# Capped attention and a spatial gating block on one Trainium2 core: the low parts of the weights move from GpSimd to VectorE, and the list scheduler in the source is given that exclusion and new weights

## The chip, the cores and the metric

The kernel runs on one core of one Trainium2 chip. The metric is the device time of one execution in microseconds, as the median of several executions. The core has TensorE (PE) for matmuls, VectorE (DVE), ScalarE (ACT), GpSimd (POOL) and SyncE (SP), which here issues almost all DMAs. The profile is of one execution.

## The reference

Four batches; each has 12 attention heads over 448 positions with 64 values a head, and then a gated block on the 768 joined values.

```python
def _attn_ref(q, k, v, cap):                       # (4, 12, 448, 64) each
    scores = cap * np.tanh(scale * q @ k.T / cap)
    attn = np.exp(scores - max);  attn /= attn.sum + 1e-9
    return attn @ v

def _moe_ref(x, w_in, g_ln, w_sg, b_sg, w_out):    # x (4, 448, 768)
    h = gelu_tanh(x @ w_in)                        # 768 -> 1024
    u, v = h[..., :512], h[..., 512:]
    v_n = (v - mean) / sqrt(var + 1e-6) * g_ln
    v_s = einsum('ts,bsd->btd', w_sg, v_n) + b_sg  # 448 x 448 over positions
    return x + (u * v_s) @ w_out                   # 512 -> 768
```

`w_in` and `w_out` come as 64-bit floats and are taken apart on the chip. (The lines above are shortened from the reference; the max is taken out of the kernel's work, since the cap bounds the scores.)

## The kernel before

**Precision by splitting.** Most matmuls run in a rounded 32-bit format. Each operand is kept as a high part (a rounded copy) and a low part (the value minus that copy), and a product is three matmuls: high x high, high x low, low x high (`TERMS`). So everything that enters such a matmul costs a copy (helper `cop`, on VectorE at L323 or ScalarE at L325, whichever the scheduler chooses) and a subtraction.

**Attention.** A batch has six pairs of heads, in three groups of two pairs. `split` makes the high and low parts of q and k (L323/L325 and L525). A group has seven units: six of 128 keys of one pair, and one for the last 64 keys of both pairs. A unit is: scores on TensorE (L535, the tail unit L543) into one of two PSUM tiles `sc`; tanh (L596) and exp (L598) on ScalarE into a tile `p`; the product with v (L554, tail L564) into an accumulator `ps`; and the row sums (`den`, L479), also on TensorE. Where `SUMS` is true for the batch, VectorE first adds three units of a pair together (L615), so that a group needs three entries in `den` and not seven; two entries make one `den` operation of eight matmuls.

**The gated block of a batch, `gated(b)`.** `recip` turns `den` into reciprocals (VectorE L625 to L631). `norm` multiplies each of the six x tiles by them (a matmul L656 that spreads them, VectorE L659) and splits x (L662, L665). Then TensorE runs `hv` (v half of x @ w_in, L698), `hu` (u half, L745), `vsg` (L762) and `outp` (L784), with gelu (L679 to L686), statistics (L717 to L730, of which L722 on GpSimd) and further splits between them.

**Weights.** `decode` handles one chunk of `w_in` (twelve of 128x512) or `w_out` (eight of 128x384): a DMA of the 64-bit words into a tile `stage`, then L395 or L397, L401, L405 and L410 on VectorE or ScalarE, an integer addition on GpSimd (L415), the high copy (L422) and the low part by a subtraction on GpSimd (L423). `split_sg` does copy and subtraction (L458, GpSimd) for the four chunks of `w_sg`. No `hv` can finish before the six chunks of the v half are decoded.

**What sets the order.** The program first collects all operations with their buffers (`Plan.op`), each with a key. `Plan.run` is a list scheduler in the source: it keeps a modelled time for each engine, and takes again and again the operation that could start first; among those of one engine within 0.04 us of each other the lowest key wins. It issues the instructions in that order, so each engine's queue is fixed when the program is built, and on the chip an engine works it off in order. The modelled costs are `c_act`, `c_tt`, `c_ts`, `c_pool`, `mms`. A DMA is modelled as 0.065 us of SP. GpSimd's hold on VectorE enters only in one place: a VectorE operation marked `fast` is lengthened by at most 0.36 us while GpSimd is busy. Keys come from the constants at the top: attention unit i has `akey(i)` (5.0 + 0.43 i for the first 42 units, then a pitch of 1.82 from 132.71); the gated blocks start at `MOE + MOE_SPAN * b`.

Of the kernel before, what the change touches and what calls it, by code (L numbers as in the profile page):

```python
# [22 lines left out]
FIRST_PITCH = 0.43  # L23
SECOND = 132.71
ATT_PITCH = 1.82
MOE = 103.44
MOE_SPAN = 49.4
SWITCH = 5.7
SIZES = (3, 7, 4, 3, 14)
RS = 19  # L30
G_CAP = 3
ACT_SH = 71.76
DVE_SH = 22.15
# [9 lines left out]
SG_FETCH = (50.0, 3.0)  # L43
GELU = 9.94
NORM = 53.2
RECIP = 20.57
VAL = 4.3
DEN = 0.0
DEC_AHEAD = 12.02

LAT = {
    ("pe", "pe"): 0.0, ("pe", "act"): 0.04, ("pe", "dve"): 0.04, ("pe", "sp"): 0.03,
# [21 lines left out]
def c_pool(n):  # L74
    return 0.0028 * n + 0.15
# [55 lines left out]
class Plan:  # L131
# [35 lines left out]
    def run(self):  # L167
        engines = ("pe", "act", "dve", "pool", "sp")
        free = dict.fromkeys(engines, 0.0)
        cand = {e: [] for e in engines}  # L170
        mode, wire, left = None, 0.0, len(self.ops)

        def ready(o):
            for e in o.engs:
                cand[e].append(o)

        for o in self.ops:
            if not o.npred:
                ready(o)
        while left:  # L180
            best = None
            for e in engines:
                ests, f = [], free[e]
# [16 lines left out]
                pick = min(  # L200
                    (x for x in ests if x[0] <= first),
                    key=lambda x: (x[1].key + (SWITCH if e == "pe" and x[1].mode != mode else 0.0)
                                   + ({"act": ACT_SH, "dve": DVE_SH}[e] if len(x[1].engs) > 1 else 0.0), x[1].num))
                if best is None or pick[0] < best[0]:
                    best = (*pick, e)
            if best is None:
                raise RuntimeError(f"stuck with {left} left")
            t, o, e = best
            cost, fn = o.engs[e]
            for k in o.engs:  # L210
                cand[k].remove(o)
            for b in o.alloc:
                b.pool.take(b)
            if e == "pe":
                if mode != o.mode:
# [14 lines left out]
            left -= 1  # L230
            for s in o.weak:
                s.npred -= 1
                s.ready = max(s.ready, t)
                if not s.npred:
                    ready(s)
            for s in o.succ:
                s.npred -= 1
                s.ready = max(s.ready, t if e == "pe" and "pe" in s.engs else max(end + LAT[e, k] for k in s.engs))
                if not s.npred:
                    ready(s)  # L240
            for b in o.bufs:
                b.left -= 1
                b.end = max(b.end, end)
                if not b.left and b.pool is not None:
                    b.pool.give(b)
        return max(free.values())
# [3 lines left out]
def kernel(  # L250
# [61 lines left out]
    ps_p = Pool([pp.tile([128, 512], FP32, name=f"ps{i}") for i in range(3)], {"g": G_CAP})  # L312
# [26 lines left out]
    def load(out, in_, buf, size, key, rd=()):  # L339
        return op("sp", 0.065, lambda: nc.sync.dma_start(out=out(), in_=in_), rd=rd, wr=[buf], key=key, size=size)  # L340

    def akey(i):
        n = 2 * NU * NG
        return i * FIRST_PITCH + 5.0 if i < n else SECOND + (i - n) * ATT_PITCH

# [6 lines left out]
    load(lambda: cap_sb, cap.partition_broadcast(128), k_cap, 512, 1.0)  # L352
# [25 lines left out]
    def decode(name, ws, src, c, sl, key):  # L378
# [10 lines left out]
        op("sp", 0.065, lambda: nc.sync.dma_start(out=st.t[:, :2 * n].bitcast(U64), in_=src),  # L389
# [23 lines left out]
        def whole():  # L413
# [39 lines left out]
    def split_sg(c):  # L453
# [12 lines left out]
    def attention(b):  # L466
# [3 lines left out]
        total = NG * (NU if not SUMS[b] else 3)  # L470
# [22 lines left out]
        def group(gi):  # L493
# [7 lines left out]
            pav = [Buf(ps_p, cls="a") for _ in pairs]  # L501
# [5 lines left out]
            def fetch(s):  # L507
                for n, src in enumerate((q2, k2)):
                    op("sp", 0.065, lambda s=s, n=n, src=src: nc.sync.dma_start(
                        out=raw[s].t[:, n, :], in_=src[b, pairs[s]]),  # L510
                       wr=[(raw[s], n)], key=base - FETCH_G + s * 3, size=128 * S * 4)

            def fetch_v(s):
                op("sp", 0.065, lambda: nc.sync.dma_start(out=v[s].t, in_=vp[b, pairs[s]]),
                   wr=[v[s]], key=base - 12 + 12 * s, size=128 * 128 * FC * 4)

            def split(s):
                key = akey(i0 + (FC + 1) * s) - SPLIT
                parts = range(2) if g == 0 and s == 0 else (slice(0, 2),)
                for n in parts:  # L520
# [4 lines left out]
                    op("dve", c_tt(cols), lambda n=n: nc.vector.tensor_tensor(  # L525
                        out=hl[s].t[:, 1, n], in0=raw[s].t[:, n], in1=f32(hl[s].t[:, 0, n]), op=ALU.subtract),
                       rd=[(raw[s], reg), (hl[s], ("h", n) if reg is not None else "h")],
                       wr=[(hl[s], ("l", n) if reg is not None else "l")], key=key)
# [50 lines left out]
            op("sp", 0.065, lambda: nc.sync.dma_start(out=vtail.t, in_=vt[b, gi]),  # L579
# [4 lines left out]
            for k, (s, c) in enumerate(units):  # L584
# [22 lines left out]
                if not SUMS[b]:  # L607
# [14 lines left out]
    def recip(b, key):  # L622
# [8 lines left out]
        op("dve", c_tt(S), lambda: nc.vector.tensor_tensor(  # L631
            out=rds[64:], in0=t.t[:64, :S], in1=f32(rds[:64]), op=ALU.subtract),
           rd=[t, (k_rds, 0)], wr=[(k_rds, 1)], key=key - RECIP)

    def gated(b):
        start = MOE + MOE_SPAN * b
# [14 lines left out]
        def norm(p):  # L653
# [8 lines left out]
            op("dve", c_tt(S), lambda: nc.vector.tensor_tensor(  # L662
                out=xl[p].t[:, :S], in0=xr[p].t, in1=f32(xh[p].t[:, :S]), op=ALU.subtract),
               rd=[xr[p], (xh[p], 0)], wr=[xl[p]], key=k)
# [27 lines left out]
        def hv(t):  # L692
# [35 lines left out]
            def lo():  # L728
# [5 lines left out]
            op("dve", c_tt(HF), lambda: nc.vector.tensor_tensor(  # L734
                out=lo(), in0=vv(), in1=f32(vh[t].t[:n]), op=ALU.subtract),
               rd=[v2, (vh[t], 0)], wr=[vl[t] if t < FC else (vh[t], 1)], key=key + 1)
# [18 lines left out]
        def vsg(f):  # L755
            ps = Buf(ps_p, cls="g")
            for c in range(NC):
# [17 lines left out]
            op("dve", c_tt(S), lambda: nc.vector.tensor_tensor(  # L775
                out=gl[f].t[:, :S], in0=uu[f].t, in1=f32(gh[f].t[:, :S]), op=ALU.subtract),
               rd=[uu[f], gh[f]], wr=[gl[f]], key=key)

        def outp(c):
# [13 lines left out]
            op("sp", 0.065, lambda: nc.sync.dma_start(out=outT[b, c], in_=x.t), rd=[x], key=key, size=128 * S * 4)  # L793
# [82 lines left out]
```

## Time and profile before

| | |
|---|---|
| median of 3 runs | 418.34 us (417.82 to 449.83) |
| the profiled execution's own time | 417.94 us |
| its span, first to last instruction | 416.2 us |
| PE busy | 391.9 us (94%), 2144 matmuls |
| DVE busy | 312.0 us (75%) |
| ACT busy | 238.6 us (57%) |
| POOL busy | 78.8 us (19%), 64 instructions |
| mean granted TensorE clock | 0.987 |

A row of instruction groups gives the line and engine, what is written and read with its shape, the count, then busy time, mean duration in ns and the idle time of the engine just before them with what ended it. A windows row gives busy us and instruction counts of each engine in a stretch. A row of the chain gives start, length and the work that the end of the kernel hung on at that moment. Matmuls overlap, so a matmul's mean duration is longer than its share of the engine's time; the chain's merged rows give that share. Likewise two VectorE instructions in a row overlap by some 0.08 us.

### The profile page before, as it was taken

To read this page: it belongs to the slowest core of one execution; us is meant where nothing else is said; L and a number is where in the kernel's file an instruction comes from. 1 tells how busy PE (TensorE), PEld (TensorE's weight loads), DVE (VectorE), ACT (ScalarE), POOL (GpSimd) and SP (SyncE) were. 2 spreads that over 40 slices of the span, in tenths; PEclk is the share of its full clock that TensorE was granted. 3 is DMA by queue.
4 is the path that set the end of the run, shared out by engine and by line. 5 is a ranking of instruction groups with operands and counts; after the bars stand their busy time and mean duration, and the time that the engine had idled before them with its cause. 6 is when DMAs were issued, how large, how long until landed. Compare 5 with 4: busy or idle time off the path is not lost.

```text
span 416.2 us, 5637 instructions
## 1 busy us (share of the span) xinstructions
PE 391.9 (94%) x2144; PEld 258.3 (62%) x2144; DVE 312.0 (75%) x515; ACT 238.6 (57%) x314; POOL 78.8 (19%) x64
## 2 busy tenths in 40 slices
PE   4988979689899999999999999999999999999996
PEld 1333424223467994856657747568557989889995
DVE  2899999989999789755686985962289967278551
ACT  5998897929577545485476575752833423134210
POOL 0443472856612322100010000000000100011000
PEclk9999999869999999999999999999999999999999
DMA  7992560605212122241030030211000001100012
GB/s 251 338 346 89 166 228 16 206 8 164 63 45 83 44 72 66 84 130 52 21 106 8 20 113 20 63 46 66 2 22 0 2 0 60 53 22 2 1 45 89
DMA packets 20140, 33.42 MB, mean 80 GB/s; under 512 B 2960, under 2 KB 17424, under 8 KB 20112
## 3 DMA queue, kind: packets, MB, share of 16 engines
q1 hardware_dynamic: 20112, 33.05, 24.3%
q8 instruction: 17, 0.28, 0.3%
q14 instruction: 11, 0.09, 0.1%
HBM read 27.53 MB, written 5.51 MB: 79 GB/s over the span
## 4 chain that ended last, share of the span: by engine, by line
PE 67%; DVE 18%; issue 5%; DMA 4%; POOL 3%; ACT 1%; SPq 1%; DVEq 0%; ACTq 0%; POOLq 0%
PE ps L698 12%; PE ps L784 10%; PE ps L745 8%; PE ps L554 7%; PE ps L762 6%; PE sc L535 6%; PE sc L784 4%; PE sc L745 4%; PE sc L762 2%; DMA stage<-in_w_in_dram 2%; DVE stage L410 2%; POOL win L423 2%; DVE t L628 2%; PE den L479 2%; PE sc L698 2%
## 5 line engine op out<-in xcount | busy, mean ns | idle before, releaser
L596 ACT ACTIVATE p<-sc,qsc 128x896 f32<-128x896 f32 x84 | 81.2, 1008 | 35.1 <-PE sc L535 29.8
L598 ACT ACTIVATE p<-p,cap_sb 128x896 f32<-128x896 f32 x84 | 84.1, 1046 | 0.2
L554 PE MATMUL ps<-p,v 128*64 128x448 f32 x276 | 59.2, 553 | 0.8 <-ACT p L598 0.7
L535 PE MATMUL sc<-hl 64*128 64x448 f32 x432 | 58.8, 393 | 0.5 <-ACT p L596 0.5
L535 PEld LDWEIGHTS sc<-hl 64*128 64x128 f32 x432 | 37.2, 188 | 34.3 <-ACT p L596 13.5
L615 DVE TENSOR_TENSOR p<-p,p 128x896 f32<-128x896 f32 x36 | 43.2, 1200 | 7.8 <-PE ps L554 6.5
L722 POOL TENSOR_TENSOR sm<-sm,pw 128x1 f32<-128x1 f32 (+1 forms) x16 | 9.3, 580 | 209.9 <-DVE sm L719 209.9
L698 PE MATMUL ps<-win,rg 128*128 128x512 f32 x187 | 47.7, 397 | 0.0
L745 PE MATMUL ps<-rg,win 128*128 128x448 f32 x202 | 45.0, 367 | 0.0
L784 PE MATMUL ps<-rg,wout 128*128 128x448 f32 x198 | 44.2, 369 | 0.0
L415 POOL TENSOR_TENSOR stage<-stage 128x512 int32<-128x512 int32 (+1 forms) x20 | 30.4, 1518 | 62.4 <-DVE stage L410 46.8
L698 PEld LDWEIGHTS ps<-win,rg 128*128 128x128 f32 x187 | 34.7, 188 | 9.8 <-issue 1.4
L745 PEld LDWEIGHTS ps<-rg,win 128*128 128x128 f32 x202 | 37.7, 188 | 4.8 <-issue 0.7
L784 PEld LDWEIGHTS ps<-rg,wout 128*128 128x128 f32 x198 | 36.8, 188 | 5.7 <-issue 1.7
L554 PEld LDWEIGHTS ps<-p,v 128*64 128x64 f32 x276 | 16.9, 137 | 32.6 <-issue 23.6
L679 ACT ACTIVATE t<-ps 128x448 f32<-128x448 f32 (+1 forms) x22 | 12.5, 568 | 38.0 <-PE ps L698 28.6
L479 PE MATMUL den<-p,ones_sb 128*32 128x448 f32 x192 | 27.1, 567 | 4.8 <-DVE t L625 3.1
L684 ACT ACTIVATE t<-t 128x448 f32<-128x448 f32 (+2 forms) x32 | 19.4, 605 | 20.7 <-DVE t L681 20.6
L681 DVE SCALAR_TENSOR_TENSOR t<-t,ps 128x448 f32<-128x448 f32 (+1 forms) x22 | 14.2, 645 | 22.6 <-ACT t L679 22.5
L423 POOL TENSOR_TENSOR win<-stage,win 128x512 fp32r<-128x512 f32 x12 | 25.4, 2120 | 25.7 <-DVE win L323 23.6
L525 DVE TENSOR_TENSOR hl<-raw,hl 128x896 fp32r<-128x896 f32 (+1 forms) x25 | 26.8, 1075 | 1.5 <-ACT hl L325 1.3
L762 PE MATMUL ps<-wsg,rg 128*128 128x448 f32 x111 | 24.4, 367 | 0.0
(117 smaller groups left out, 536.0 us busy)
## 6 DMA issues: line engine op xcount, KB each, us to landing
stage<-in_w_in_dram SPq DMA_DIRECT2D x12, 512.0 KB, 5.6
raw<-in_q_dram SPq DMA_DIRECT2D x24, 224.0 KB, 3.6
raw<-in_k_dram SPq DMA_DIRECT2D x24, 224.0 KB, 3.9
out_dram<-x SPq DMA_DIRECT2D x24, 224.0 KB, 1.9
v<-in_vp_dram SPq DMA_DIRECT2D x24, 192.0 KB, 2.7
stage<-in_w_out_dram SPq DMA_DIRECT2D x8, 384.0 KB, 3.2
u<-in_w_sgT_dram SPq DMA_DIRECT2D x4, 224.0 KB, 7.5
vt<-in_vt_dram SPq DMA_DIRECT2D x12, 64.0 KB, 2.3
```

What stands on the lines that cost most here:

```text
L415: nc.gpsimd.tensor_tensor(out=a.bitcast(I32), in0=a.bitcast(I32), in1=hi, op=ALU.add)
L423: op("pool", c_pool(n), lambda: nc.gpsimd.tensor_tensor(out=ws[1][:, c, sl], in0=words()[2], in1=f32(ws[0][:, c, sl]), op=ALU.subtract), r ...
L479: nc.tensor.matmul(out=den.t[32 * j:32 * j + 32, :S], lhsT=ones_sb[:, kind, NP - 1 - kind - p:NP + 31 - kind - p], rhs=src.t[:, h, :], sta ...
L535: nc.tensor.matmul(out=sc.t[:, h, :S], lhsT=hl[s].t[rows, w, 1, 128 * c - 128:128 * c], rhs=hl[s].t[rows, m, 0], start=(k == 0), stop=(k = ...
L554: nc.tensor.matmul(out=pav[s].t[64 * h:64 * h + 64, :S], lhsT=v[s].t[:, 128 * (c - 1) + 64 * h:128 * (c - 1) + 64 * h + 64], rhs=p.t[:, h, ...
L596: op("act", c_act(2 * S, True, True), lambda p=p, sc=sc: nc.scalar.activation(out=p.t, in_=sc.t[:, :, :S], func=ACTF.Tanh, scale=qsc), rd= ...
L598: op("act", c_act(2 * S, False, True), lambda p=p: nc.scalar.activation(out=p.t, in_=p.t, func=ACTF.Exp, scale=cap_sb), rd=[k_cap], wr=[p] ...
L615: op("dve", c_tt(2 * S), lambda a=a, p=p: nc.vector.tensor_tensor(out=a.t, in0=a.t, in1=p.t, op=ALU.add), rd=[p], wr=[a], key=akey(i) + 5.0)
L698: nc.tensor.matmul(out=ps.t[:, :HF], lhsT=(xl if a else xh)[c].t[:, t * 128:t * 128 + 128], rhs=win[w][:, c, HF:], start=(c == 0 and k == ...
L745: nc.tensor.matmul(out=ps.t[:, :S], lhsT=win[w][:, c, f * 128:(f + 1) * 128], rhs=(xl if a else xh)[c].t[:, :S], start=(c == 0 and k == 0) ...
L762: nc.tensor.matmul(out=ps.t[:, :S], lhsT=(vl if a else vh)[c].t[:, f * 128:(f + 1) * 128], rhs=wsg[w][:, c, :], start=(c == 0 and k == 0), ...
L784: nc.tensor.matmul(out=ps.t[:, :S], lhsT=wout[w][:, f, c * 128:(c + 1) * 128], rhs=(gl if a else gh)[f].t[:, :S], start=(f == 0 and k == 0 ...
```

## The change

The two low-part subtractions of the weights go to VectorE, through a new helper `sub` that also serves the subtractions already there. The scheduler now treats a marked VectorE operation and a GpSimd operation as exclusive, in both directions, and gets new costs for GpSimd and for a DMA issue. Two DMAs of k at the start go to ScalarE's queue. `SUMS` is now per group, the attention keys per batch, the start and span of each gated block per batch, and nearly all other constants, buffer counts among them, have new values.

```diff
-FIRST_PITCH = 0.43
-SECOND = 132.71
-ATT_PITCH = 1.82
-MOE = 103.44
-MOE_SPAN = 49.4
-SWITCH = 5.7
-SIZES = (3, 7, 4, 3, 14)
+ATT = ((-2.4, 2.04), (48.67, 2.63), (116.23, 4.59), (190.0, 4.4))
+GATED = ((68.97, 119.99), (182.94, 117.55), (316.07, 26.93), (334.53, 60.0))
+SWITCH = 6.88
+SIZES = (3, 5, 4, 3, 18)
...
-SUMS = (True, False, True, True)
-RETIRE = (8, 8, 8, 8, 8, 0)
-IN_V = (22.2, 15.3)
-IN_U = (36.4, 5.3)
-OUT_W = (136.5, 12.2)
-SG_W = (57.5, 5.9)
-FETCH_W = 38.96
-FETCH_G = 38.23
-SPLIT = 19.18
...
+SUMS = (0, 1, 0, 0, 1, 0, 1, 1, 1, 1, 1, 1)
+RETIRE = (11, 8, 7, 8, 8, 0)
+IN_V = (33.7, 15.2)
+IN_U = (51.1, 6.6)
+OUT_W = (145.9, 10.0)
+SG_W = (64.9, 4.1)
+FETCH_W = 8.26
+FETCH_G = 8.66
+SPLIT = 37.4
...
+ISSUE = 0.45
...
 def c_pool(n):
-    return 0.0028 * n + 0.15
+    return 0.00235 * n + 0.09
...
+        port = {"dve": 0.0, "pool": 0.0}
...
                 for o in cand[e]:
                     t = o.ready if o.ready > f else f
+                    if o.fast and e in port:
+                        t = max(t, port["dve" if e == "pool" else "pool"])
...
             else:
-                if e == "dve" and o.fast:
-                    cost += 0.6 * max(0.0, min(free["pool"], t + 0.6) - t)
                 end = t + cost
+                if o.fast and e in port:
+                    port[e] = end - 0.135
                 free[e] = end - OVERLAP[e]
...
-    ps_p = Pool([pp.tile([128, 512], FP32, name=f"ps{i}") for i in range(3)], {"g": G_CAP})
+    ps_p = Pool([pp.tile([128, 512], FP32, name=f"ps{i}") for i in range(3)], {"g": G_CAP, "b": 2})
...
+    def sub(out, a, b, n, rd, wr, key):
+        op("dve", c_tt(n), lambda: nc.vector.tensor_tensor(out=out(), in0=a(), in1=b(), op=ALU.subtract),
+           rd=rd, wr=wr, key=key, fast=True)
...
-        op("pool", c_pool(n), whole, rd=[(st, "h")], wr=[(st, "a")], key=key)
+        op("pool", c_pool(n), whole, rd=[(st, "h")], wr=[(st, "a")], key=key, fast=True)
         cop(lambda: ws[0][:, c, sl], lambda: words()[2], n, [(st, "a")], [(w, 0)], key)
-        op("pool", c_pool(n), lambda: nc.gpsimd.tensor_tensor(
-            out=ws[1][:, c, sl], in0=words()[2], in1=f32(ws[0][:, c, sl]), op=ALU.subtract),
-           rd=[(st, "a"), (w, 0)], wr=[(w, 1)], key=key)
+        sub(lambda: ws[1][:, c, sl], lambda: words()[2], lambda: f32(ws[0][:, c, sl]), n,
+            [(st, "a"), (w, 0)], [(w, 1)], key)
...
-        op("pool", c_pool(S), lambda: nc.gpsimd.tensor_tensor(
-            out=wsg[1][:, c, :], in0=u.t, in1=f32(wsg[0][:, c, :]), op=ALU.subtract),
-           rd=[u, (w, 0)], wr=[(w, 1)], key=SG_W[0] + SG_W[1] * c)
+        sub(lambda: wsg[1][:, c, :], lambda: u.t, lambda: f32(wsg[0][:, c, :]), S,
+            [u, (w, 0)], [(w, 1)], SG_W[0] + SG_W[1] * c)
...
                 for n, src in enumerate((q2, k2)):
-                    op("sp", 0.065, lambda s=s, n=n, src=src: nc.sync.dma_start(
+                    eng = "act" if n and not g else "sp"
+                    queue = nc.scalar if n and not g else nc.sync
+                    op(eng, ISSUE, lambda s=s, n=n, src=src, queue=queue: queue.dma_start(
                         out=raw[s].t[:, n, :], in_=src[b, pairs[s]]),
...
                     def to_ps(bf):
                         ps_p.caps = {}
-                        for z in range(2):
-                            ps_p.add(bf.end, bf.t[:, z, :])
+                        ps_p.add(bf.end, bf.t[:, 0, :])
                         return True
...
-                if not SUMS[b]:
+                if not SUMS[g]:
...
-                        out=a.t, in0=a.t, in1=p.t, op=ALU.add), rd=[p], wr=[a], key=akey(i) + 5.0)
+                        out=a.t, in0=a.t, in1=p.t, op=ALU.add), rd=[p], wr=[a], key=akey(i) + 5.0, fast=True)
...
-        start = MOE + MOE_SPAN * b
+        start, span = GATED[b]
```

## Rows read from the trace of the kernel before

**Rows 1.** Windows, four stretches: engine busy us (instructions), TensorE clock, DMA share, GB/s.
```profile
0.00:60.00 60.00, 50.95 (x314) 19.80 (x314) 50.07 (x76) 52.26 (x59) 24.88 (x14) 1.00 0.73 242
60.00:112.00 52.00, 42.10 (x277) 15.96 (x278) 49.23 (x67) 36.25 (x45) 29.88 (x21) 0.90 0.28 88
112.00:310.00 198.00, 197.11 (x1076) 133.61 (x1074) 144.10 (x249) 121.17 (x161) 20.17 (x23) 1.00 0.18 58
```

**Rows 2.** Chain that ended last, pieces in which TensorE runs without a gap.
```profile
133.38 14.72 PE ps L745 x72
...
239.09 0.91 PE sc L543 x8
...
246.58 0.91 PE ps L564 x8
...
248.29 0.89 PE den L479 x8
249.18 2.41 PE ps L554 x12
251.58 1.43 PE sc L535 x12
...
363.60 7.69 PE ps L698 x33
```

**Rows 3.** What TensorE waited for before 112 us: total, times, longest.
```profile
PE ps L656 <- DVE x L659: 6.2, 1, 6.2
PE sc L543 <- DMA raw<-in_k_dram: 5.2, 1, 5.2
PE den L479 <- DVE t L625: 3.1, 1, 3.1
```

**Rows 4.** Windows of 10 us around the longest wait, same columns as rows 1.
```profile
80.00:90.00 10.00, 4.69 (x21) 1.43 (x23) 10.00 (x13) 3.68 (x5) 6.96 (x5) 0.55 0.14 50
90.00:100.00 10.00, 10.00 (x70) 3.87 (x68) 7.46 (x15) 7.77 (x9) 5.68 (x4) 0.94 0.26 74
```

**Rows 5.** Instruction groups on GpSimd, whole span.
```profile
L415 POOL TENSOR_TENSOR stage<-stage 128x512 int32<-128x512 int32 (+1 forms) x20 | 30.4, 1518 | 62.4 <-DVE stage L410 46.8 <-DVE stage L405 15.2 <-issue 0.4
...
L423 POOL TENSOR_TENSOR win<-stage,win 128x512 fp32r<-128x512 f32 x12 | 25.4, 2120 | 25.7 <-DVE win L323 23.6 <-ACT win L325 2.1
...
L423 POOL TENSOR_TENSOR wout<-stage,wout 128x384 fp32r<-128x384 f32 x8 | 8.3, 1040 | 4.5 <-ACT wout L325 3.2 <-DVE wout L323 1.3
...
L458 POOL TENSOR_TENSOR wsg<-u,wsg 128x448 fp32r<-128x448 f32 x4 | 5.7, 1439 | 0.0
```

**Rows 6.** Timeline, all engines: a subtraction on GpSimd among VectorE's instructions (start, length).
```profile
27.43 2.07 POOL L423 TENSOR_TENSOR win<-stage,win 128x512 fp32r<-128x512 f32 x1 [2.77 <-DVE win L323]
...
28.28 2.17 DVE L615 TENSOR_TENSOR p<-p,p 128x896 f32<-128x896 f32 x1
...
30.91 1.08 DVE L615 TENSOR_TENSOR p<-p,p 128x896 f32<-128x896 f32 x1
```

**Rows 7.** Instruction groups on VectorE, 0 to 112 us.
```profile
L615 DVE TENSOR_TENSOR p<-p,p 128x896 f32<-128x896 f32 x12 | 17.1, 1427 | 0.2 <-ACT p L596 0.2
...
L410 DVE SCALAR_TENSOR_TENSOR stage<-stage 128x512 int32<-128x512 int32 (+1 forms) x14 | 13.1, 941 | 0.1
L401 DVE TENSOR_SCALAR stage<-stage 128x512 f32<-128x512 f32 (+1 forms) x14 | 10.6, 756 | 0.6 <-POOL win L423 0.6
L405 DVE TENSOR_SCALAR stage<-stage 128x512 int32<-128x512 int32 (+1 forms) x14 | 9.4, 675 | 0.0
```

**Rows 8.** VectorE's timeline: the decode's steps where GpSimd is not at work.
```profile
71.33 0.41 DVE L401 TENSOR_SCALAR stage<-stage 128x512 f32<-128x512 f32 x1
...
90.20 0.41 DVE L405 TENSOR_SCALAR stage<-stage 128x512 int32<-128x512 int32 x1
...
91.21 0.68 DVE L410 SCALAR_TENSOR_TENSOR stage<-stage 128x512 int32<-128x512 int32 x1
...
107.06 0.55 DVE L410 SCALAR_TENSOR_TENSOR stage<-stage 128x384 int32<-128x384 int32 x1
```

More of the change, by code (lines that the diff above doesn't have):

```diff
@@ L170, in run @@
         cand = {e: [] for e in engines}
-        mode, wire, left = None, 0.0, len(self.ops)
+        mode, wire, left, last = None, 0.0, len(self.ops), 0.0
+        port = {"dve": 0.0, "pool": 0.0}
         def ready(o):
@@ L230, in run @@
             left -= 1
+            last = max(last, end)
             for s in o.weak:
@@ L245, in run @@
                     b.pool.give(b)
-        return max(free.values())
+        return last
 @with_exitstack
@@ L339, in load @@
     def load(out, in_, buf, size, key, rd=()):
-        return op("sp", 0.065, lambda: nc.sync.dma_start(out=out(), in_=in_), rd=rd, wr=[buf], key=key, size=size)
+        return op("sp", ISSUE, lambda: nc.sync.dma_start(out=out(), in_=in_), rd=rd, wr=[buf], key=key, size=size)
     def akey(i):
-        n = 2 * NU * NG
-        return i * FIRST_PITCH + 5.0 if i < n else SECOND + (i - n) * ATT_PITCH
+        at, pitch = ATT[i // (NU * NG)]
+        return at + pitch * (i % (NU * NG))
     BOTH = ("dve", "act")
@@ L388, in decode @@
         st.on_free = freed
-        op("sp", 0.065, lambda: nc.sync.dma_start(out=st.t[:, :2 * n].bitcast(U64), in_=src),
+        op("sp", ISSUE, lambda: nc.sync.dma_start(out=st.t[:, :2 * n].bitcast(U64), in_=src),
            wr=[(st, "w")], key=key - FETCH_W, size=n * 128 * 8)
@@ L469, in attention @@
         per = {}
-        total = NG * (NU if not SUMS[b] else 3)
+        total = sum(3 if s else NU for s in SUMS[NG * b:NG * b + NG])
         def den_op(units, key):
@@ L500, in group @@
             vtail = Buf(vt_p)
-            pav = [Buf(ps_p, cls="a") for _ in pairs]
+            pav = [Buf(ps_p, cls="a" if b < 2 else "b") for _ in pairs]
             x = [Buf(x_p) for _ in pairs]
@@ L508, in fetch @@
                 for n, src in enumerate((q2, k2)):
-                    op("sp", 0.065, lambda s=s, n=n, src=src: nc.sync.dma_start(
+                    eng = "act" if n and not g else "sp"
+                    queue = nc.scalar if n and not g else nc.sync
+                    op(eng, ISSUE, lambda s=s, n=n, src=src, queue=queue: queue.dma_start(
                         out=raw[s].t[:, n, :], in_=src[b, pairs[s]]),
-                       wr=[(raw[s], n)], key=base - FETCH_G + s * 3, size=128 * S * 4)
+                       wr=[(raw[s], n)], key=base - FETCH_G + s * 3 if g else -99.0 + s, size=128 * S * 4)
             def fetch_v(s):
-                op("sp", 0.065, lambda: nc.sync.dma_start(out=v[s].t, in_=vp[b, pairs[s]]),
+                op("sp", ISSUE, lambda: nc.sync.dma_start(out=v[s].t, in_=vp[b, pairs[s]]),
                    wr=[v[s]], key=base - 12 + 12 * s, size=128 * 128 * FC * 4)
@@ L524, in split @@
                         [(raw[s], reg)], [(hl[s], ("h", n) if reg is not None else "h")], key)
[L525 to L528, printed above, removed]
+                    sub(lambda n=n: hl[s].t[:, 1, n], lambda n=n: raw[s].t[:, n], lambda n=n: f32(hl[s].t[:, 0, n]), cols,
+                        [(raw[s], reg), (hl[s], ("h", n) if reg is not None else "h")],
+                        [(hl[s], ("l", n) if reg is not None else "l")], key)
             def scores(i, s, c, sc):
@@ L578, in group @@
                 fetch_v(s)
-            op("sp", 0.065, lambda: nc.sync.dma_start(out=vtail.t, in_=vt[b, gi]),
+            op("sp", ISSUE, lambda: nc.sync.dma_start(out=vtail.t, in_=vt[b, gi]),
                wr=[vtail], key=base - 6, size=128 * 128 * 4)
@@ L630, in recip @@
            rd=[t], wr=[(k_rds, 0)], key=key - RECIP)
-        op("dve", c_tt(S), lambda: nc.vector.tensor_tensor(
-            out=rds[64:], in0=t.t[:64, :S], in1=f32(rds[:64]), op=ALU.subtract),
-           rd=[t, (k_rds, 0)], wr=[(k_rds, 1)], key=key - RECIP)
+        sub(lambda: rds[64:], lambda: t.t[:64, :S], lambda: f32(rds[:64]), S, [t, (k_rds, 0)], [(k_rds, 1)], key - RECIP)
     def gated(b):
-        start = MOE + MOE_SPAN * b
+        start, span = GATED[b]
         at = [0.0]
@@ L644, in pe @@
             at[0] += cost
-            op("pe", cost, fn, rd=rd, wr=wr, key=start + MOE_SPAN * at[0] / full, mode="G")
+            op("pe", cost, fn, rd=rd, wr=wr, key=now(), mode="G")
         def now():
-            return start + MOE_SPAN * at[0] / full
+            return start + span * at[0] / full
         xh, xl = [Buf(r_p) for _ in range(NP)], [Buf(r_p) for _ in range(NP)]
@@ L661, in norm @@
             cop(lambda: xh[p].t[:, :S], lambda: xr[p].t, S, [xr[p]], [(xh[p], 0)], k)
-            op("dve", c_tt(S), lambda: nc.vector.tensor_tensor(
-                out=xl[p].t[:, :S], in0=xr[p].t, in1=f32(xh[p].t[:, :S]), op=ALU.subtract),
-               rd=[xr[p], (xh[p], 0)], wr=[xl[p]], key=k)
+            sub(lambda: xl[p].t[:, :S], lambda: xr[p].t, lambda: f32(xh[p].t[:, :S]), S,
+                [xr[p], (xh[p], 0)], [xl[p]], k)
             op("dve", c_tt(TL), lambda: nc.vector.tensor_tensor(
@@ L733, in hv @@
             cop(lambda: vh[t].t[:n], vv, HF, [v2], [(vh[t], 0)], key + 1)
-            op("dve", c_tt(HF), lambda: nc.vector.tensor_tensor(
-                out=lo(), in0=vv(), in1=f32(vh[t].t[:n]), op=ALU.subtract),
-               rd=[v2, (vh[t], 0)], wr=[vl[t] if t < FC else (vh[t], 1)], key=key + 1)
+            sub(lo, vv, lambda: f32(vh[t].t[:n]), HF, [v2, (vh[t], 0)], [vl[t] if t < FC else (vh[t], 1)], key + 1)
         uu = {}
@@ L774, in vsg @@
             cop(lambda: gh[f].t[:, :S], lambda: uu[f].t, S, [uu[f]], [gh[f]], key)
-            op("dve", c_tt(S), lambda: nc.vector.tensor_tensor(
-                out=gl[f].t[:, :S], in0=uu[f].t, in1=f32(gh[f].t[:, :S]), op=ALU.subtract),
-               rd=[uu[f], gh[f]], wr=[gl[f]], key=key)
+            sub(lambda: gl[f].t[:, :S], lambda: uu[f].t, lambda: f32(gh[f].t[:, :S]), S,
+                [uu[f], gh[f]], [gl[f]], key)
         def outp(c):
@@ L792, in outp @@
                 out=x.t, in0=x.t, in1=ps.t[:, :S], op=ALU.add), rd=[ps], wr=[x], key=key)
-            op("sp", 0.065, lambda: nc.sync.dma_start(out=outT[b, c], in_=x.t), rd=[x], key=key, size=128 * S * 4)
+            op("sp", ISSUE, lambda: nc.sync.dma_start(out=outT[b, c], in_=x.t), rd=[x], key=key, size=128 * S * 4)
         for t in range(NC):
```

29 lines of the change are left out of this document (14 added, 15 removed).

## The prediction, on record before the result

> **What bounds the kernel now.** I read the windows first: they say where TensorE, 94% busy over the span, isn't busy. From 112 to 310 us it stands still for 0.9 us in 198; before 112 us it is idle for 9.1 us of the first 60 and 9.9 us of the next 52 [rows 1]. The table's 24.3 us of idle time is therefore nearly all at the front (19.0 us); some 4.4 us are left for the end.
>
> Busy time hides a second loss, so I price the work by pieces of the chain in which TensorE runs without a gap [rows 2]. Scores of a unit: 1.43 / 2 = 0.715 us; values 2.41 / 3 = 0.803; the tail unit's scores and values 0.91 each; a `den` operation 0.89. A group is 6 x (0.715 + 0.803) + 1.82 = 10.9 us, twelve groups 131. `den` has 5 + 11 + 5 + 5 = 26 operations (9 entries with sums, 21 without, two to an operation): 23. A 448-column matmul is 14.72 / 72 = 0.204, a 512-column one 7.69 / 33 = 0.233; a gated block has 188 + 6 of the first and 66 of the second: 55 us, four 220. The sum is 374 us; the span is 42 longer. The first 112 us hold only six groups, 16 `den` operations and a few norms: 65.4 + 14.2 + about 1.2 = 81 us of work in 112. So 31 of the 42 us are lost there: 19.0 as idle time, 12 as busy time longer than the work.
>
> Why, say the waits: 5.2 us until the first k has landed, 6.2 us for VectorE's first multiplication of x in `norm`, 3.1 us for VectorE's reading of `den` [rows 3]. Behind the 6.2 us the granted clock is 0.55 in one window and 0.94 in the next [rows 4]; the first of those is near the lower of the clock's two levels (1.2 of 2.4 GHz), after TensorE had stood still. That costs 4.69 x 0.45 + 10.0 x 0.06 = 2.7 us of the 12. VectorE is busy 50.1 of 60 and 49.2 of 52 us [rows 1], and ScalarE only 36 of the latter 52: between 60 and 112 us VectorE sets the pace.
>
> VectorE's time is itself stretched. A subtraction on GpSimd starts at 27.43 and ends at 29.50; the L615 issued at 28.28 takes 2.17 us, the next one 1.08 [rows 6]. The first ends 0.95 us after GpSimd, as if it had waited for the whole of it. Over the first 112 us L615 takes 17.1 us where 12 x 1.08 = 13.0 would do, L410 13.1 where 12 x 0.68 + 2 x 0.55 = 9.3 would, L401 10.6 and L405 9.4 where 14 x 0.41 = 5.7 would [rows 6 to 8]: 16.5 us of stretching in these four lines. The old scheduler allows at most 0.36 us for one such meeting, and none for L615, which isn't marked; so its fixed order for TensorE assumes results that come later, and TensorE stands behind a norm matmul while other work waits in its queue.
>
> **The change part by part**, against the profiled execution's own 417.94 us (span 416.2, with 1.7 around it; 0.4 under the median).
>
> *The subtractions.* GpSimd loses 25.4 + 8.3 + 5.7 = 39.4 of its 78.8 us [rows 5]. VectorE gains 24 instructions. At 512 columns I take 0.68 us, at 384 0.55, both from L410, which also reads two operands [rows 8], and 0.62 between them for 448: 8.2 + 4.4 + 2.5 = 15.1 us. Before 112 us it is the 12 of `w_in`, 4 of `w_sg` and 1 of `w_out`: 11.2 us onto the engine that is nearly full. Against that, 17 of the 31 GpSimd operations there (35 less 4 memsets at the start) [rows 1] go. 16.5 us over 31 is 0.53 each, so 9.0 us of stretching go and 7.5 stay. Bounds: no relief (0) if the 14 integer additions that stay block as much as all did, the whole 16.5 if the new order avoids every meeting.
>
> The Trainium skill speaks against this part: "Perfetto Trace Analysis", section Optimizing Scalar/DVE Operations, says that work may be moved off VectorE when VectorE is saturated, to GpSimd too, and the change goes the other way. It adds that a move between those two may not help, as they share a read port. By the first sentence alone the front gets longer by the 11.2 us; rows 6 side with the second. It is the slower rival below.
>
> *Sums per group.* Eight groups are summed and not nine: 4 L615 fewer, 4.3 us at 1.08. All of it is at the front: batches 0 and 1 have 8 where they had 12. TensorE gets `den` operations 9 + 9 + 5 + 5 = 28, two more: +1.8 us. Together VectorE's front changes by 11.2 - 9.0 - 4.3 = -2.1 us. I take -2.1 on the path, since VectorE paces that stretch.
>
> *The scheduler's model and the new keys.* Nothing is added to an engine; the order changes. What can go are the 9.3 us of waits on VectorE [rows 3] and the 2.7 us of clock. VectorE stays nearly full, so I take three quarters of the waits, -7.0, and the 2.7 whole; bounds: 0 and -12.0. Gated block 0 gets a start key of 69 instead of 103, and attention of batch 1 a pitch of 2.63 instead of 0.43, so that TensorE has both kinds of work from about 75 us on, if the decode keeps up. The 12 us of stretched busy time less 2.7 leave 9; I take a third, -3.0 (bounds 0 and -9).
>
> *The opening.* k goes out on ScalarE's queue beside q. ScalarE's two DMA issues stand ahead of its work but cost nothing, as it waits for the first k anyway. No row shows an issue there; the bounds are -0.9, two issues fewer ahead of the last k at the 0.45 us that the new scheduler gives one, and +0.9, the two issues in the way of the first activation. I take -0.5.
>
> *At no cost.* One PSUM bank is given over after the last scores, from two tiles, instead of two each: a product of 12 matmuls lasts 12 x 0.204 = 2.4 us and its reading by VectorE 0.6, so five accumulators cover each other; if not, some 2 us in the last 100. Five `p` tiles instead of seven hold back ScalarE only where `den` is late. The GpSimd additions now wait in the plan for VectorE; queued behind them are only more additions and the small L722, and a late addition delays one chunk of weights.
>
> Sum: -2.1 - 7.0 - 2.7 - 3.0 - 0.5 + 1.8 = -13.5. 417.94 - 13.5 = **404.4 us**; its own range is 399 to 409.5.
>
> **The rivals.**
>
> *More than that.* The plan is now right in detail, all waits on VectorE and all stretched time go: 9.3 + 2.7 + 9 + 2.1 + 0.5 - 1.8 = 21.8, so 396 us. For it: after 112 us TensorE has almost no gap, so a good order suffices. Against: VectorE has 97 us of work for the front.
>
> *Half of it.* VectorE stays the pace of the front, TensorE's waits only move; the 2.1 and the 0.5 come, a third of the waits and of the clock (4.0), and 1.8 goes: 4.8, so 413 us. For it: 99.3 of 112 us busy, and hv needs all six chunks of the v half, whose keys still run to 110 after 99 before. This is also the case in which the scheduler's exclusion isn't the chip's, and the order gains nothing by it.
>
> *Slower: VectorE becomes the bound of the decode.* Place: the chunks of `w_in` before the first hv. The 14 additions left block as much as the 31 operations did, since each stands between steps of VectorE for the same chunk. Price: 11.2 - 4.3 = +6.9 on a front without slack, +1.8 for `den`, and the hole of rows 4 grows with it, its clock loss once more (+2.7): 429 us. It decides if the mean of L401, L405 and L410 before the first hv stays near 0.75, 0.68 and 0.94 us. Against it stand rows 6: two operations cannot block each other where one is gone.
>
> **How the numbers follow.** Forecast 0.45, more 0.17, half 0.22, slower 0.16. A measurement here can tell 2% from no change, that is 410.0 and 426.7 us around the median. Faster is the forecast, but for 0.02 of it, and the first rival: 0.60. Slower by over 2% is the last rival, but for 0.02: 0.14. The rest, 0.26, is within. Low end 395: just past the first rival. High end 421: past the half case and part of the way to 429; it leaves out some 0.05 below and 0.14 above.
>
> **What would show each step.** GpSimd busy near 39 us or under; 24 subtractions of weights on VectorE at 0.55 to 0.7 us; L401 and L405 near 0.5; 32 L615 and 208 `den` matmuls (16 more); VectorE's total at 305 to 312 us. TensorE's first hv well before 111 us, its idle time before 112 us near 11 us, no window with the clock at 0.55, the stretch from 112 to 310 us still without gaps. I am wrong if waits on VectorE in the first 112 us still sum to 9 us, if the middle has new ones (the two value accumulators of a group held longer by the wider pitch of batches 2 and 3 leave one `ps` for the gated work), or if the end, from 310 us on, gets more than its 4.4 us of idle time.

## The result

The changed kernel takes 406.83 us (median of 4 runs, 406.67 to 407.81), 0.9728 times the kernel before, 95% interval 0.9700 to 0.9755. The forecast was 404.4 us, its own range 399 to 409.5. The profiled execution took 406.84 us; its span is 405.1 us, 11.1 shorter. The 449.83 us in the table of before is a slow run, and no ratio here uses it.

The rows below answer to [rows 1], in the same stretches (windows, columns as there).

```profile
0.00:60.00 60.00, 53.22 (x358) 20.97 (x362) 48.01 (x83) 53.88 (x63) 11.37 (x10) 1.00 0.74 243
60.00:112.00 52.00, 51.51 (x298) 25.45 (x290) 48.45 (x88) 48.25 (x66) 15.17 (x10) 1.00 0.29 92
112.00:310.00 198.00, 197.21 (x1076) 129.66 (x1075) 149.57 (x248) 116.77 (x154) 11.25 (x14) 1.00 0.18 57
```

TensorE's idle time before 112 us fell from 19.0 to 7.3 us. Over the whole span it fell by 12.2 (24.3 to 12.1), while its busy time rose by 1.0 (391.9 to 393.0): that is the 11.1 us. VectorE is as full at the front as before (96.5 of 112 us after 99.3); GpSimd went from 54.8 to 26.5 us there.

What TensorE waited for before 112 us comes next. [rows 3] has the three longest waits before the change; the same view has two more on VectorE:

```profile
PE den L479 <- DVE p L615: 1.7, 2, 1.5
PE ps L698 <- DVE x L659: 1.3, 1, 1.3
```

So the waits on VectorE came to 6.2 + 3.1 + 1.7 + 1.3 = 12.3 us, and not 9.3. After the change the view has three rows; the window below them is the one that held the longest wait [rows 4]:

```profile
PE sc L547 <- DMA raw<-in_q_dram: 6.4, 1, 6.4
PE sc L539 <- ACT p L599: 0.5, 2, 0.3
PE ps L558 <- ACT p L601: 0.2, 1, 0.2
```
```profile
80.00:90.00 10.00, 10.00 (x53) 6.41 (x53) 10.00 (x19) 10.00 (x16) 1.84 (x1) 1.00 0.25 73
```

All waits on VectorE are gone, and with them the window at clock 0.55. What is left is the opening, and that is 1.2 us longer. Between 80 and 90 us three engines are busy for all of it.

VectorE's groups before 112 us (answer to [rows 7]; the lines moved by three to five, and `sub` is L354 for all subtractions):

```profile
L415 DVE SCALAR_TENSOR_TENSOR stage<-stage 128x512 int32<-128x512 int32 (+1 forms) x15 | 9.9, 663 | 0.1
L354 DVE TENSOR_TENSOR win<-stage,win 128x512 fp32r<-128x512 f32 x12 | 9.3, 777 | 0.1
L618 DVE TENSOR_TENSOR p<-p,p 128x896 f32<-128x896 f32 x8 | 9.3, 1160 | 0.4 <-ACT p L601 0.4
L410 DVE TENSOR_SCALAR stage<-stage 128x512 int32<-128x512 int32 (+1 forms) x15 | 7.1, 476 | 0.0
L406 DVE TENSOR_SCALAR stage<-stage 128x512 f32<-128x512 f32 (+1 forms) x15 | 6.4, 427 | 0.0
...
L354 DVE TENSOR_TENSOR wsg<-u,wsg 128x448 fp32r<-128x448 f32 x4 | 3.5, 870 | 0.1
```

The decode's steps are back at about the length that they have alone [rows 8]: against those, L415, L410, L406 and L618 carry 0.1 + 0.9 + 0.2 + 0.7 = 1.9 us of stretching, after 16.5. The subtractions take 0.78 and 0.87 us on average, after the 0.68 and 0.62 that I put in. Their medians are 0.68 and 0.63; one of each, at 76.20 and 17.68 us, meets an addition on GpSimd and takes 1.80 and 1.60, so some 2.1 us more of stretching lie here. GpSimd's additions are as stretched as before, 1.77 us on average before 112 us after 1.68 (the first row is of the kernel before):

```profile
L415 POOL TENSOR_TENSOR stage<-stage 128x512 int32<-128x512 int32 (+1 forms) x14 | 23.5, 1678 | 31.3 <-DVE stage L410 31.0 <-issue 0.4
...
L420 POOL TENSOR_TENSOR stage<-stage 128x512 int32<-128x512 int32 (+1 forms) x14 | 24.6, 1766 | 73.4 <-DVE stage L415 43.7 <-DMA g_sb<-in_g_ln_dram 17.0 <-DMA stage<-in_w_in_dram 10.7
```

The matmuls of hv (L698) among TensorE's groups before 112 us:

```profile
L698 PE MATMUL ps<-win,rg 128*128 128x512 f32 x58 | 14.7, 399 | 0.0
...
L698 PE MATMUL ps<-win,r 128*128 128x512 f32 x8 | 2.8, 434 | 0.0
```

There are 66 of them, after 3 before the change. The same six groups of attention units are done too, so TensorE has nearly 15 us more work behind it at 112 us (63 matmuls at 0.233). Only 11.1 us of it come out at the end: the 16 added `den` matmuls cost 1.8 by the prediction's price, and by the same prices the rest, under 2 us, is lost behind 112 us. It is lost as busy time, since idle time there fell slightly (5.3 to 4.8 us).

### The profile page after: what moved, and what is told of

Its sections match the earlier page's. It is cut to its first block, busy times and chain, and to the rows that moved or that the text cites. A ratio compares the mean times of both kernels' runs of the same rounds, so it can differ in the third digit from the quotient of the medians.

```text
span 405.1 us, 5652 instructions
## 1 busy us (share of the span) xinstructions
PE 393.0 (97%) x2160; PEld 257.4 (64%) x2160; DVE 301.9 (75%) x525; ACT 243.3 (60%) x324; POOL 41.1 (10%) x40
## 4 chain that ended last, share of the span: by engine, by line
PE 71%; ACT 11%; DVE 11%; issue 3%; POOL 1%; DMA 1%; SPq 0%; ACTq 0%; POOLq 0%; DVEq 0%
PE ps L781 10%; PE ps L743 9%; PE ps L698 8%; PE ps L558 8%; PE ps L760 7%; PE sc L539 7%; PE sc L781 5%; ACT p L599 5%; ACT p L601 4%; PE sc L698 4%; PE sc L743 3%; PE den L482 2%; PE sc L547 2%; PE sc L760 2%; PE ps L568 2%
## 5 line engine op out<-in xcount | busy, mean ns | idle before, releaser
L558 PE MATMUL ps<-p,v 128*64 128x448 f32 x288 | 62.8, 554 | 0.2 <-ACT p L601 0.2
L539 PE MATMUL sc<-hl 64*128 64x448 f32 x432 | 57.8, 391 | 0.5 <-ACT p L599 0.5
L743 PE MATMUL ps<-rg,win 128*128 128x448 f32 x216 | 49.3, 369 | 0.0
L698 PE MATMUL ps<-win,rg 128*128 128x512 f32 x183 | 46.8, 400 | 0.0
L743 PEld LDWEIGHTS ps<-rg,win 128*128 128x128 f32 x216 | 40.1, 188 | 7.0 <-issue 3.4
L781 PE MATMUL ps<-rg,wout 128*128 128x448 f32 x189 | 42.0, 368 | 0.0
L698 PEld LDWEIGHTS ps<-win,rg 128*128 128x128 f32 x183 | 33.7, 188 | 12.0 <-issue 3.1
L781 PEld LDWEIGHTS ps<-rg,wout 128*128 128x128 f32 x189 | 35.1, 188 | 5.6 <-issue 2.2
L618 DVE TENSOR_TENSOR p<-p,p 128x896 f32<-128x896 f32 x32 | 35.3, 1105 | 3.7 <-ACT p L601 2.2
L760 PE MATMUL ps<-wsg,rg 128*128 128x448 f32 x131 | 29.9, 372 | 0.0
L354 DVE TENSOR_TENSOR hl<-raw,hl 128x896 fp32r<-128x896 f32 (+1 forms) x25 | 26.9, 1081 | 1.1 <-ACT hl L326 0.9
L760 PEld LDWEIGHTS ps<-wsg,rg 128*128 128x128 f32 x131 | 24.3, 188 | 5.1 <-DVE p L618 1.4
```

Of the source, the lines that this page charges most:

```text
L354: op("dve", c_tt(n), lambda: nc.vector.tensor_tensor(out=out(), in0=a(), in1=b(), op=ALU.subtract), rd=rd, wr=wr, key=key, fast=True)
L539: nc.tensor.matmul(out=sc.t[:, h, :S], lhsT=hl[s].t[rows, w, 1, 128 * c - 128:128 * c], rhs=hl[s].t[rows, m, 0], start=(k == 0), stop=(k = ...
L558: nc.tensor.matmul(out=pav[s].t[64 * h:64 * h + 64, :S], lhsT=v[s].t[:, 128 * (c - 1) + 64 * h:128 * (c - 1) + 64 * h + 64], rhs=p.t[:, h, ...
L698: nc.tensor.matmul(out=ps.t[:, :HF], lhsT=(xl if a else xh)[c].t[:, t * 128:t * 128 + 128], rhs=win[w][:, c, HF:], start=(c == 0 and k == ...
L743: nc.tensor.matmul(out=ps.t[:, :S], lhsT=win[w][:, c, f * 128:(f + 1) * 128], rhs=(xl if a else xh)[c].t[:, :S], start=(c == 0 and k == 0) ...
L760: nc.tensor.matmul(out=ps.t[:, :S], lhsT=(vl if a else vh)[c].t[:, f * 128:(f + 1) * 128], rhs=wsg[w][:, c, :], start=(c == 0 and k == 0), ...
```

## The experiments

**The three large parts, one or two at a time.** The change has three parts that could each carry the gain: the move of the subtractions, the scheduler's treatment of GpSimd (called the model below), and the constants. The first four kernels take them apart.

*Move only.* The kernel before, `op("pool", c_pool(n), ... nc.gpsimd ...)` made `op("dve", c_tt(n), ... nc.vector ...)` in L423 and L458.

```diff
-        op("pool", c_pool(n), lambda: nc.gpsimd.tensor_tensor(
+        op("dve", c_tt(n), lambda: nc.vector.tensor_tensor(
             out=ws[1][:, c, sl], in0=words()[2], in1=f32(ws[0][:, c, sl]), op=ALU.subtract),
```

> The kernel before with one edit: the 24 weight subtractions run on VectorE; scheduler and constants are the old ones. Theory (the move itself is worth little, the order most): 414 to 419 us, VectorE's waits still in the way of TensorE before 112 us (5 us or more). Rival A (the move is the gain, by less stretching on VectorE): 407 to 411 us. Rival B (VectorE is full, the move costs): 425 us or more.

Measured: 413.54 us, ratio 0.9898 (0.9875 to 0.9921). Under the theory's range by a little: the move alone is worth 4.3 us, with a plan that the old scheduler made anew. The two old waits of 6.2 and 3.1 us are gone, though the scheduler knows nothing new. All waits on VectorE before 112 us fall from 12.3 to 3.6 us (L615 2.6 after 1.7, L659 1.0 after 1.3), under the theory's 5; those on ScalarE grow, the largest to 3.0. Rival B, the slower one of the prediction, falls: VectorE's busy time before 112 us is 99.8 us after 99.3, though 18 subtractions have come to it. GpSimd's additions pay for that here, 2.52 us after 1.68 on average. VectorE's L401 shows its own relief, 0.46 us on average after 0.76 [rows 7]:

```profile
L401 DVE TENSOR_SCALAR stage<-stage 128x512 f32<-128x512 f32 (+1 forms) x14 | 6.4, 455 | 0.0
```

*Model only.* The kernel before with the new exclusion, marks, GpSimd cost and DMA issue cost.

```diff
+                    if o.fast and e in port:
+                        t = max(t, port["dve" if e == "pool" else "pool"])
...
-                if e == "dve" and o.fast:
-                    cost += 0.6 * max(0.0, min(free["pool"], t + 0.6) - t)
                 end = t + cost
+                if o.fast and e in port:
+                    port[e] = end - 0.135
```

> The kernel before with the scheduler's new treatment of GpSimd alone (exclusion in both directions, the marks, the new GpSimd and DMA issue costs); the subtractions stay on GpSimd, the constants are old. Theory: with right start times TensorE's order fits, its waits on VectorE before 112 us fall under 4 us, 409 to 414 us. Rival A: 416 to 419 us, as the stretching stays. Rival C (only the new constants matter): 417 to 420 us.

Measured: 429.11 us, ratio 1.0266 (1.0234 to 1.0299), slower by over 10 us where I expected a gain. The theory in this form falls. Before 112 us TensorE is busy 99.9 us, 6.9 more than before the change, and its waits on VectorE fall from 12.3 to 5.8 us (not under 4, as I expected), so the front did get better; but the middle and the end got gaps (windows, columns as in rows 1):

```profile
112.00:310.00 198.00, 192.12 (x1034) 130.06 (x1028) 136.91 (x234) 116.67 (x158) 23.39 (x25) 0.99 0.19 60
...
330.00:340.00 10.00, 7.74 (x36) 6.14 (x35) 4.91 (x11) 2.25 (x4) 0.54 (x1) 1.00 0.00 0
```

*Model and move.* Both edits above; constants old.

> The kernel before with the subtractions on VectorE and the new treatment of GpSimd in the scheduler; constants old. Theory: 408 to 412 us, most of the gain without any new constant. Rival A: the same as the move alone. Rival C: 416 us or more, as gated block 0 still starts near 111 us.

Measured: 420.86 us, ratio 1.0076 (1.0055 to 1.0098). Again worse than the move alone. Before 112 us the model does what it was meant to: no wait on VectorE is left, and idle time is 10.6 us, after 14.8 with the move alone. The loss comes later. From 112 to 310 us 3.2 us are idle, and from 310 us on 11.0 of 110.6, after 0.9 and 4.4 of 106.2 in the kernel before.

*New constants and move, old model.* The changed kernel with the exclusion and the marks taken out again.

> The changed kernel with the old treatment of GpSimd in the scheduler (no exclusion, the old lengthening, old GpSimd cost, old marks); subtractions on VectorE, constants new. Theory: TensorE gets waits on VectorE of 3 us or more before 112 us again, 409 to 415 us. Rival C (the constants are the gain): 406 to 408 us.

Measured: 416.08 us, ratio 0.9951 (0.9929 to 0.9974). 9.3 us over the changed kernel, and 2.5 over the move alone: the constants without the model don't carry the gain. (The new constants with neither model nor move were not run.) Idle time before 112 us is 13.6 us, and the waits are there, though I named the wrong engine:

```profile
PE sc L545 <- DMA raw<-in_q_dram: 6.3, 1, 6.3
PE sc L537 <- ACT p L597: 4.0, 3, 2.5
PE ps L696 <- ACT rg L324: 1.5, 1, 1.5
```

So far, model and constants are only good together. Two questions followed: what goes wrong at the end when the model is new and the constants old, and whether the constants are a lucky pick for one single plan.

**What the end hangs on.** In both kernels with gaps at the end, TensorE stops in the middle of products into a score tile `sc`; all waits of TensorE that the view has from 310 us on, 6.9 us in each, are for matmuls into `sc`. The old code hands over both halves of such a tile as accumulators once the last scores are done; the change hands over one. I had put that edit at no cost.

*The changed kernel with both halves.*

```diff
-                        ps_p.add(bf.end, bf.t[:, 0, :])
+                        for z in range(2):
+                            ps_p.add(bf.end, bf.t[:, z, :])
```

> The changed kernel, but after the last scores both halves of a score tile are given over as accumulators again. If writing one half waits until VectorE has read the other: TensorE waits on VectorE or ScalarE in products into sc after 280 us, 3 to 8 us in all, 410 to 415 us. If the halves are independent: 406 to 407 us, no such waits.

Measured: 412.36 us, ratio 0.9850 (0.9824 to 0.9876): 5.5 us over the changed kernel (5.1 by the ratios), near half of the gain. The profile is of its fastest run, 410.80 us: TensorE waits 3.3 us there for readers of `sc`, in seven places, and its span is 3.9 us longer. The timeline of its end, rows that touch `sc`:

```profile
315.80 0.54 ACT L680 ACTIVATE t<-sc 128x448 f32<-128x448 f32 x1 [1.27 <-PE sc L744]
...
316.40 0.87 PE L744 MATMUL sc<-rg,win 128*128 128x448 f32 x3 [0.63 <-ACT t L680]
317.38 0.62 DVE L682 SCALAR_TENSOR_TENSOR t<-t,sc 128x448 f32<-128x448 f32 x1 [1.29 <-PE sc L744]
...
318.05 1.49 PE L744 MATMUL sc<-rg,win 128*128 128x448 f32 x6 [0.78 <-DVE t L682]
319.65 0.62 DVE L687 SCALAR_TENSOR_TENSOR u<-t,sc 128x448 f32<-128x448 f32 x1 [0.93 <-PE sc L744]
...
320.32 5.15 PE L744 MATMUL sc<-rg,win 128*128 128x448 f32 x24 [0.79 <-DVE u L687]
```

A product of 18 matmuls is cut into 3, 3, 6 and 6 (the first 3 follow a whole product without a gap, and the last 6 are followed by one, so the row says 24). Before each later piece TensorE waits for a reader of `sc`, and each reader waits for TensorE's piece before it. No reader can want a product that is only a sixth done, so what is read is the other half: in this program the order is kept for the tile as a whole, not for its halves. Whether this costs much depends on the plan, since the kernel before, with both halves, has only three such waits, of 0.4 us at most.

*Model, move and old constants, with one half.* The same edit the other way, on the kernel of 420.86 us.

> Old constants, subtractions on VectorE, new treatment of GpSimd (420.9 us), and only one half of each score tile given over at the end. If the halves caused the end's gaps (some 7 us of idle time more than before): 413 to 415 us, no better than the move alone with the old scheduler. If a truer model helps with old constants as soon as the end is mended: 410 us or less. If the end's gaps have another cause: 420 to 421 us.

Measured: 411.82 us, ratio 0.9828 (0.9788 to 0.9869; the runs spread from 409.8 to 414.7). The halves cost 9 us there, and no wait on a reader of `sc` is left at the end. With the end mended, the true model is no longer harmful. Against the move alone (0.9875 to 0.9921) the intervals just miss each other, but the runs of this kernel spread by 5 us, so a gain of some 2 us by the model with old constants is likely and not settled. The remaining 5.0 us to the changed kernel come from the constants, which also outweigh the longer opening (the old one is used here). In its profile, of the slowest of its runs, the middle still waits for chunks of `w_out`, and the clock fell in one stretch before 112 us.

**The constants.** *Control: one constant nudged.*

```diff
-SPLIT = 37.4
+SPLIT = 36.4
```

> Control: the changed kernel with one constant moved (SPLIT 36.4 instead of 37.4), so that the scheduler makes another plan under the same model. If the plan is robust: 406 to 408 us. If the constants pick one plan out of many that differ by chance: 409 us or more, with waits of TensorE in new places.

Measured: 407.08 us, ratio 0.9712 (0.9684 to 0.9740). As a control it says little, for it is hardly another plan: in the two traces TensorE's 2160 matmuls come in the same order by line and tile, and VectorE and ScalarE swap one pair of instructions each, between 232 and 236 us. It shows that a plan gives the same time again, to 0.25 us. Whether the constants are one lucky draw is tested by the next two kernels, in which TensorE's order differs from its 45th and its 215th matmul on.

*Sums as before*, `SUMS = (1, 1, 1, 0, 0, 0, 1, ...)`.

> The changed kernel with the sums on VectorE as before (batch 0 all groups, batch 1 none). My sum gave the new choice 4.3 us less of VectorE and 1.8 us more of TensorE: 407 to 410 us. If where VectorE's load lies in the first 112 us is what counts: 411 us or more.

Measured: 407.26 us, ratio 0.9735 (0.9717 to 0.9753). VectorE is busy 100.8 of the first 112 us instead of 96.5, and it costs 0.4 us, within the intervals. The first hv comes at 86.1 us instead of 79.2.

*Old keys of attention and gated blocks*, `5.0 + 0.43 i` and so on.

> The changed kernel with the old keys of attention units and gated blocks; all else new. If the earlier start of gated block 0 carries the gain: 413 us or more, first hv near 105 us, TensorE waiting on ScalarE or VectorE at the front again. If the other constants do: 407 to 410 us.

Measured: 406.91 us, ratio 0.9733 (0.9706 to 0.9759). The first hv moves from 79.2 to 95.5 us and nothing is lost (the first row is of the changed kernel; shortest, median and longest in ns, then first and last start):

```profile
L698 PE MATMUL ps<-win,r x15: 390/396/503, 79.2 to 352.3; 128*128 128x512 f32 x15
...
L698 PE MATMUL ps<-win,r x17: 392/396/497, 95.5 to 361.2; 128*128 128x512 f32 x17
```

So the constants aren't one lucky draw, and 16 us of the gated block's earlier start are not where the gain is. (With the old keys it still starts 16 us before the 111.4 of the kernel before, so what those are worth isn't shown.) TensorE still nearly always finds something ready, with 8.9 us of idle time before 112 us after 7.3; that this is what counts is argued. Which of the other constants carry the 5 us (fetch and split leads, norm lead, buffer counts, accumulator limits) I have not tried.

**The engine of the subtractions under the new plan.** *Same order, subtractions issued to GpSimd.* Only the call is changed; every other engine keeps its order.

> The changed kernel with every engine's order as planned, but the 24 weight subtractions issued to GpSimd at their place in the plan. Isolates the engine of the subtractions under the new order. If their engine matters (stretching): 412 us or more, L406, L410 and L415 longer again, and waits of TensorE on VectorE come back. If it hardly does: 406 to 409 us.

Measured: 413.19 us, ratio 0.9860 (0.9831 to 0.9888). L406 and L410 before 112 us, to be held against the rows of the result:

```profile
L406 DVE TENSOR_SCALAR stage<-stage 128x512 f32<-128x512 f32 (+1 forms) x15 | 10.3, 689 | 0.0
...
L410 DVE TENSOR_SCALAR stage<-stage 128x512 int32<-128x512 int32 (+1 forms) x14 | 9.2, 657 | 0.1
```

The stretching is back, waits on VectorE before 112 us come to 3.9 us, and idle time there is 10.7 us after 7.3.

*Subtractions on GpSimd, plan made anew for that.*

> The changed kernel with the 24 weight subtractions on GpSimd and the plan made for that, with the exclusion modelled. If a true model is what counts: 408 to 412 us. If the constants fit only the plan for which they were found: 415 us or more, as the model alone gave 429 us with the old constants.

Measured: 408.31 us, ratio 0.9742 (0.9712 to 0.9772). With a plan that knows of it, the slower placement costs only 1.5 us, and the intervals overlap. L406 and L410 are at 0.46 and 0.47 us there, while L415 (0.86) and the sums (1.32) are still stretched: the stretching has not gone, but TensorE's order is made for it. Its waits on VectorE before 112 us come to 1.2 us, and idle time there is 8.0.

**The opening.** *k on SyncE's queue again*, order unchanged.

```diff
-                    queue = nc.scalar if n and not g else nc.sync
+                    queue = nc.sync
```

> The changed kernel, same order of all engines, the first two k loads on SyncE's queue instead of ScalarE's. The first matmul started at 6.4 us instead of 5.2. If the second queue did that, by letting four transfers share the DMA engines instead of landing one after the other: 0.5 to 1.2 us faster, 405.6 to 406.3 us, first matmul near 5.2 us. If not: 406.8 us.

Measured: 406.33 us, ratio 0.9698 (0.9673 to 0.9722); its span is 404.2, 0.9 under the changed kernel's. What TensorE waited for at the start:

```profile
PE sc L547 <- DMA raw<-in_k_dram: 5.2, 1, 5.2
```

This is the fastest of all kernels here; it beats the changed one by 0.5 us in the median, which the intervals don't separate, and by 1.2 us in the wait itself.

## Why the prediction was right, and where it was not

*Bound and place.* Right: the loss lay before 112 us, and nearly all of the gain is idle time there (11.7 of the 12.2 us).

*The rivals.* None of them came: VectorE did not become the bound of the decode, TensorE's waits did not merely move, and not all of the loss went. Half of the first one did: all waits on VectorE are gone, the stretched busy time is not.

*The subtractions.* Right in sign, the sizes off twice, in opposite ways. I let 7.5 us of stretching stay, in four lines; 1.9 stayed. I priced the 16 subtractions of `w_in` and `w_sg` at 10.6 us; they took 12.8, since two of them met GpSimd; the price of one alone was right. With 4 L615 fewer, VectorE's front came out 2.8 us shorter, forecast 2.1. The path is another matter: the move alone gave 4.3 us, twice the term, as it removed waits by itself; under the new plan it is worth 6.4 us at a fixed order and 1.5 with the plan redone. The Trainium skill's advice that I weighed ("Perfetto Trace Analysis", Optimizing Scalar/DVE Operations, to unload a saturated VectorE onto GpSimd), read as a rule, would make this move a loss; the kernel with the move alone shows a gain of 1.0%, with VectorE as full as before. The caution that follows it there, and with which rows 6 sided, is what the trace bears out.

*Sums per group.* The term was too large: -4.3 at VectorE and +1.8 at TensorE make -2.5, and the kernel with the old sums is 0.4 us slower, within the intervals. Which of the two parts was smaller on the path isn't shown.

*The scheduler's order.* I read only the three longest rows of the waits: those on VectorE were 12.3 us and not 9.3. They went whole, where I took 7.0; no window before 112 us has a clock under 1.00 now, so the clock's 2.7 went as said. The reason that I gave is only half of it: a true model lets the order fit, but not by itself. With the old constants it made the kernel slower (by 7.3 us beside the move, where the half tiles cost 9), and with the new constants the old model left 9.3 us.

*A third of the stretched busy time, -3.0.* This step failed. Before 112 us the work is now 95.8 us (six groups 65.4, 15.5 `den` operations 13.8, 66 hv matmuls 15.4, norms 1.2) and TensorE busy 104.7: 8.9 us over, after 9.3 without the clock's share. So 0.4 went and not 3.0. The earlier start of the gated block, from which I expected it, moved first hv by 32 us; at least the last 16 of them are worth nothing. What stretches TensorE's busy time there stays open. (Of my 81 us for the front before the change the `den` part was too high, 120 matmuls and not 16 x 8; six score matmuls and three of hv that I left out make up for it.)

*The opening, -0.5.* Wrong sign: the first matmul starts 1.2 us later, outside the bound of +0.9 that I gave.

*The bank at no cost.* Right as a difference to the kernel before, which has waits of 0.4 us at most there, and wrong as a judgement of the edit: with five accumulators TensorE has no wait after 310 us, as I said, but what the edit takes away is a wait between halves, 5.5 us with this plan. I asked what one accumulator fewer costs, not what two in one tile cost.

*The sum.* By terms, on the span (forecast 402.7, measured 405.1): the waits on VectorE gave 5.3 us more than forecast and other waits 0.6 more. Missing are 2.1 of VectorE's shorter front, 2.6 of the stretched time, 1.7 of the opening, and some 1.9 are lost behind 112 us: 402.7 - 5.9 + 8.3 = 405.1. The 2.1 was counted twice, for a VectorE that paces the front reaches TensorE only through its waits, and those were a term of their own. The clock's and the `den` term stand at their estimates, and the last of the losses is what the others leave over. That misses of both signs nearly cancel is luck.

## What to carry to other kernels

Where a planner in the source fixes each engine's queue, its model of costs and its constants are one thing: change one and the other may have to be found again, so neither can be judged alone (here the old constants with the new model lost 9 us by a third thing, the half tiles). Read the control's order too: a nudged constant that leaves the order as it was tests nothing. Take a long part of a change back out of the finished kernel, and not only into the old one: parts that look free there (half a tile not used) can hold near half of the gain. And two operations that shut each other out should be counted as one engine before work is moved between the two.

## What was not expected of the hardware

Two DMA queues at the start were slower than one. With k on ScalarE's queue beside q on SyncE's, all four issues are out by 2.1 us instead of 3.0, yet the first matmul starts at 6.4 us instead of 5.2, and the 512 bytes of `cap`, issued first, reach VectorE at 5.13 instead of 3.86 us:

```profile
0.73 0.89 ACTq L514 DMA_DIRECT2D raw<-in_k_dram  x2
0.73 0.38 SPq L341 DMA_DIRECT2D cap_sb<-in_cap_dram  x1
...
1.18 0.89 SPq L514 DMA_DIRECT2D raw<-in_q_dram  x2
...
2.11 0.43 SPq L519 DMA_DIRECT2D v<-in_vp_dram  x1
...
5.13 0.15 DVE L360 TENSOR_SCALAR qsc<-cap_sb 128x1 f32<-128x1 f32 x1 [4.26 <-DMA cap_sb<-in_cap_dram]
...
6.41 2.67 PE L547 MATMUL sc<-raw 64*64 64x448 f32 x8 [6.41 <-DMA raw<-in_q_dram]
```

With k back on SyncE's queue:

```profile
3.06 0.43 SPq L519 DMA_DIRECT2D v<-in_vp_dram  x1
...
3.86 0.15 DVE L360 TENSOR_SCALAR qsc<-cap_sb 128x1 f32<-128x1 f32 x1 [3.00 <-DMA cap_sb<-in_cap_dram]
...
5.21 1.72 PE L547 MATMUL sc<-raw 64*64 64x448 f32 x3 [5.21 <-DMA raw<-in_k_dram]
```

That the transfers share the DMA engines and so finish together, and not one after the other, would explain it; it is argued from these rows only. They leave a second reading: with two queues the first v is issued at 2.11 us instead of 3.06, so it may be v that q shares with, and no run here tells the two apart.
